# Fused attention and expert layer: the first group's keys cast and turned tile by tile, and a score visit moved ahead of the value pass

## The chip, the cores and the metric

The kernel runs on one core of a Trainium2 chip. The metric is the device time of one execution, in microseconds (us). Engines: PE (TensorE, matmuls), DVE (VectorE), ACT (ScalarE), POOL (GpSimd, here also the queue of most loads) and SP (SyncE, the queue of the first loads and of the stores). A matmul's weight load is listed apart, as PEld.

## The reference

The inputs q, k and v have shape 8 x 12 x 448 x 64 (batch, heads, sequence, head dimension), in float32. Attention uses a sigmoid in place of a softmax; its output goes through an expert layer with a gated hidden width of 2048:

```python
scores = scale * np.matmul(q, k.transpose(0, 1, 3, 2)) - np.log(S)
attn = 1.0 / (1.0 + np.exp(-scores))
attn_out = np.matmul(attn, v)
x = attn_out.transpose(0, 2, 1, 3).reshape(B * S, H * D)      # 3584 x 768
h = x @ w_in                                                  # 768 -> 2048
out = (h * (1.0 / (1.0 + np.exp(-beta * h)))) @ w_out         # 2048 -> 768
```

## The kernel before, in words

**Tiling.** The 12 heads of a batch form three groups of four heads; a group g holds its queries and keys as one tile `raws[g]` of 128 partitions (4 heads x 32 rows), two halves (queries, keys) and 14 chunks of 64 columns. A DVE transpose in 32 x 32 blocks of 32-bit words (L191 to L210) turns queries into `qT[g]` and keys into `kT[g]`, with pairs of fp16 numbers as words. The 448 keys of a head are three tiles of 128 (jt 0, 1, 2) and a last one of 64 (jt 3, `JF`); chunk c of the first twelve belongs to tile c mod 3, so a key tile is four chunks of 64 numbers, three chunks apart. A slot is two heads; a group has two slots.

**The opening** (L708 to L810, a schedule written out by hand: each engine runs its instructions in the order of the program). Two SP loads bring the first half of group 0's queries and all of its keys as float32 into the still unused tile `gt` (L723); everything else comes over POOL's queue, cast to fp16 by the DMA: queries and keys of groups 1 and 2, the values of batch 0 (L136, L143), the second halves of the queries, then the weights w_in (L153). DVE casts and turns group 0's queries (L747, L196). Of its keys ACT casts the second 448 columns (L749) and DVE the first (L750), and one transpose turns tiles 0 to 2 (384 words, L204), another the last tile (64 words, L208).

`half_visit(g, c0, second)` (L256) makes the scores of one half of the queries (224 columns from c0) of one group: with `second` 0 the key tiles 0 and 1, with 1 the tiles 2 and 3. It takes two score tiles (one for each slot, two PSUM banks each) out of a pool of three, runs 16 matmuls (L218) that go tile by tile, and two sigmoids on ACT (`weigh`, L230) write the weights. `attend(g, c0, n, part)` (L279) multiplies these weights by the values: 8 matmuls a slot (L291) into one PSUM bank a slot, out of two banks that `bank` (L89) gives out, the least recently used first; a DVE copy then writes `xT` (L300) and frees the bank. `double_v_last` (L145) is a DVE copy that the value pass needs. `idle_units` (L738) are matmuls of 512 columns on zeros, whose result nobody reads.

The order is: 10 idle units and one of 256 columns; six half visits for the first query half (groups 0, 1, 2), with 4, 4, 4, 4 and 2 idle units between them; `double_v_last`; the transpose of the second query half of group 0; then `attend(0)`, half visit (0, second query half, 0), `attend(1)`, half visit (0, second query half, 1), the other query transposes, and `attend(2)` slot by slot (L767 to L781). Four transposes turn beta (L784). Then the score pool is closed and opened again with two tiles, which leaves four banks for the expert layer (L794, L795), whose first matmuls (`dense1`, L305, L171) need the `xT` of all six slots and sigmoids with beta (L317). From there on a written list of steps (`STEPS`) mixes the attention of later batches with the expert layer.

Of the kernel before, what the change touches and what calls it, by code (L numbers as in the profile page):

```python
# [8 lines left out]
FP32 = mybir.dt.float32  # L9
FP16 = mybir.dt.float16  # L10
# [3 lines left out]
def kernel(  # L14
# [10 lines left out]
    nc = tc.nc  # L25
# [3 lines left out]
    B, H, S, D = q.shape  # L29
    NTOK, DM = out.shape  # L30
    DFF = moe_w_in.shape[1]
    P = 128
    BLK = 32
    HQ = P // BLK
    NB = S // BLK
    PAIR = D // BLK
    JF = S // P
    KL = S - JF * P
    NF = JF * P // BLK
    NPAIR = H // 2  # L40
    QPB = H // HQ
# [5 lines left out]
    QH = S // 2  # L47
# [7 lines left out]
    vp = ctx.enter_context(tc.tile_pool(name="vp", bufs=2))  # L55
    qTp = ctx.enter_context(tc.tile_pool(name="qTp", bufs=3))
    kTp = ctx.enter_context(tc.tile_pool(name="kTp", bufs=3))
# [27 lines left out]
    def touch(i: int):  # L85
        used[i] = max(used.values()) + 1


    def bank(name: str, cols: int = S, hold=None):  # L89
        i = min((i for i in used if i not in held.values()), key=used.get)  # L90
        touch(i)
        if hold is not None:
            held[hold] = i
        pool = psum["one" if i < N_ONE else "late"]
        return pool.tile([P, cols], FP32, tag=f"one{i}", name=name)
# [12 lines left out]
    raws = {}  # L108
    vs = {}
# [19 lines left out]
    def last_base(s: int) -> int:  # L129
        return (s % 2 ^ swapped(s // 2)) * KL  # L130

    def load_v(b: int):
        vs[b] = vp.tile([P, H, JF + 1, D], FP16, tag="v16", name="v16")
        rows = v[b].rearrange("h (p c) d -> p h (c d)", c=NB)
        for i in range(HQ):
            nc.gpsimd.dma_start(  # L136
                out=vs[b][i * BLK : (i + 1) * BLK, :, 0:JF].rearrange("p h j d -> p h (j d)"),
                in_=rows[:, :, JF * i * D : JF * (i + 1) * D],
            )
        rows = v[b].rearrange("h (p c) d -> p h c d", c=NB)  # L140
        for c in range(NF, NB):
            lo = (c - NF) * BLK
            nc.gpsimd.dma_start(out=vs[b][lo : lo + BLK, :, JF], in_=rows[:, :, c])  # L143

    def double_v_last(b: int):  # L145
        nc.vector.tensor_copy(out=vs[b][KL:P, :, JF], in_=vs[b][0:KL, :, JF])

    WCH = 8
    WOUT = 2
# [30 lines left out]
    kT = {}  # L180
# [10 lines left out]
    def transpose(g: int, r: int, c0: int = 0, c1: int = NB):  # L191
        raw = raws[g][:, r]
        if r == 0:
            if g not in qT:
                qT[g] = qTp.tile([P, NB * BLK, PAIR], FP16, tag="qT", name="qT")
            nc.vector.transpose(  # L196
                out=in_order(g // QPB, qT[g][:, c0 * BLK : c1 * BLK]),
                in_=raw[:, c0:c1].rearrange("p c d -> p (c d)").bitcast(FP32),
            )
            return  # L200
        kT[g] = kTp.tile([P, S, PAIR], FP16, tag="kT", name="kT")
        to = kT[g].rearrange("p k e -> p (k e)").bitcast(FP32)
        frm = raw.rearrange("p c d -> p (c d)").bitcast(FP32).rearrange("p (c f) -> p c f", c=NB)
        nc.vector.transpose(  # L204
            out=to[:, 0 : JF * P].rearrange("p (j i q) -> p i j q", j=JF, i=HQ),
            in_=frm[:, 0:NF].rearrange("p (i j) f -> p i j f", j=JF),
        )
        nc.vector.transpose(  # L208
            out=to[:, JF * P :], in_=frm[:, NF:].rearrange("p c f -> p (c f)")
        )  # L210
# [45 lines left out]
    def half_visit(g: int, c0: int, second: int):  # L256
        slots = (2 * g, 2 * g + 1)
        scos = [score_tile() for _ in slots]
        plan = [(s, jt, sco, jt * QH) for jt in (0, 1) for s, sco in zip(slots, scos)]
        widths = [S, S]  # L260
        if second:
            plan = [(s, 2, sco, 0) for s, sco in zip(slots, scos)]
            plan += [(s, JF, scos[0], QH) for s in slots]
            widths = [S, QH]
        for i in range(0, len(plan), 2):
            for e in range(PAIR):
                for s, jt, sco, u0 in plan[i : i + 2]:
                    for hh in range(2):
                        score(sco, u0, s, jt, hh, e, c0, QH)
        homes = [None, None]  # L270
        if c0 == 0 and g < QPB - 1:
            home = outp.tile([P, 2 * S], FP32, tag="osb", name="early")
            home = home.bitcast(FP16).rearrange("p (x h s) -> p x h s", x=2, h=2)
            homes = [home[:, x] for x in range(2)]
        ats = {id(sco): weigh(sco, n, at) for sco, n, at in zip(scos, widths, homes)}
        for s, jt, sco, u0 in plan:
            at_tiles[s, jt, c0] = ats[id(sco)][:, :, u0 : u0 + QH]
# [430 lines left out]
    NH = NB // 2  # L708
# [4 lines left out]
    with tc.manual_schedule():  # L713
        raws[0] = rawp.tile([P, 2, NB, D], FP16, tag="raw", name="raw")
        wide = gt.rearrange("p a b -> p (a b)").bitcast(FP32)
        cut = NH * D
        early = [(0, 0, NH), (1, 0, NB)]
        staged = {}
        at = 0
        for r, c0, c1 in early:  # L720
            staged[r] = wide[:, at : at + (c1 - c0) * D]
            at += (c1 - c0) * D
            nc.sync.dma_start(  # L723
                out=staged[r],
                in_=(q, k)[r][0, 0:HQ].rearrange("h (p c) d -> (h p) (c d)", c=NB)[
                    :, c0 * D : c1 * D
                ],
            )
        nc.gpsimd.memset(dummy, 0.0)
        nc.scalar.activation(out=dummy, in_=dummy, func=AF.Sigmoid, bias=0.0, scale=1.0)  # L730

        still = gt[:, NDC - 1, 0:512]
        nc.vector.memset(still, 0.0)
        beta_in = sigp.tile([P, S], FP32, tag="sg", name="beta_in")[0:BLK, 0:P]
        nc.vector.memset(beta_in, 0.0)
        idle = bank("idle_ps", 512)

        def idle_units(n: int, cols: int = 512):  # L738
            for _ in range(n):
                nc.tensor.matmul(  # L740
                    idle[:, 0:cols], still[:, 0:P], still[:, 0:cols], start=True, stop=True
                )

        idle_units(10)
        idle_units(1, 256)
        raw = raws[0].rearrange("p r c d -> p r (c d)")
        nc.vector.tensor_copy(out=raw[:, 0, 0:cut], in_=staged[0])  # L747
        transpose(0, 0, 0, NH)
        nc.scalar.copy(out=raw[:, 1, cut:], in_=staged[1][:, cut:])  # L749
        nc.vector.tensor_copy(out=raw[:, 1, 0:cut], in_=staged[1][:, 0:cut])  # L750
        transpose(0, 1)
        for g in range(1, QPB):
            load_one(g, 0, 0, NH)
            load_one(g, 1)
        load_v(0)
        nc.sync.dma_start(out=beta_in[0:NDC], in_=moe_beta.rearrange("(c p) -> c p", p=P))
        for g in range(QPB - 1):
            load_one(g, 0, NH, NB)
        for c in range(WCH):
            if c == WCH // 2:  # L760
                load_one(QPB - 1, 0, NH, NB)
            load_w_in(c)
        for g in range(1, QPB):
            transpose(g, 0, 0, NH)
            transpose(g, 1)

        for g in range(QPB):  # L767
            for second in range(2):
                half_visit(g, 0, second)
                if 2 * g + second < 2 * QPB - 1:  # L770
                    idle_units(4 if g < QPB - 1 else 2)
        double_v_last(0)
        transpose(0, 0, NH, NB)
        attend(0, 0, QH)
        half_visit(0, QH, 0)
        attend(1, 0, QH)
        half_visit(0, QH, 1)
        for g in range(1, QPB - 1):
            transpose(g, 0, NH, NB)
        attend(2, 0, QH, (0,))  # L780
        attend(2, 0, QH, (1,))  # L781
        for i in range(P // BLK):
            part = slice(i * BLK, (i + 1) * BLK)
            nc.vector.transpose(out=beta_sb[part], in_=beta_in[:, part])  # L784
        load_qk(QPB)
        load_qk(QPB + 1)
        load_v(1)
        load_w_out(0, 0)
        load_w_out(1, 0)
        load_qk(QPB + 2)  # L790
        load_w_out(0, 1)
        load_w_out(1, 1)

        firsts.close()  # L794
        share_psum(ctx, seconds, 2, N_ONE, 2)  # L795
        first_half(4)
        half_visit(1, QH, 0)
        first_half(3)
        half_visit(1, QH, 1)
        transpose(2, 0, NH, NB)  # L800
        attend(0, QH, QH)
        first_half(1)
        half_visit(2, QH, 0)
        first_half(4)
        half_visit(2, QH, 1)
        attend(1, QH, QH)
        first_half(3)
        attend(2, QH, QH)
        first_half(1)
        follow(STEPS)  # L810
# [30 lines left out]
```

## Time and profile before

| | us |
|---|---|
| median of 3 runs | 368.29 (367.94 to 368.37) |
| profiled execution, device time | 368.51 |
| profiled execution, span from first to last instruction | 366.7 |
| PE busy | 361.6 |
| ACT busy | 248.7 |
| DVE busy | 271.7 |
| last landing of group 0's keys (L723), ACT and DVE start on them | 4.76 |
| first score matmul (L218) | 6.00 |
| first sigmoid (L230) | 6.66 |
| first expert matmul (L171) | 19.42 |

A line of the timeline gives the start in us from the start of the span, the busy time in us, engine, line, operation, output<-input, shapes, the number of instructions merged into it, and in brackets the idle time of the engine just before with what ended it. A line of the chain gives start, length and what the time was spent on; "issue" is time in which the engine waited for nothing that the profile shows. The granted TensorE clock is 1.000 over the span.

### The profile page before, as it was taken

To read this page: it belongs to the slowest core of one execution; us is meant where nothing else is said; L and a number is where in the kernel's file an instruction comes from. 1 tells how busy PE (TensorE), PEld (TensorE's weight loads), DVE (VectorE), ACT (ScalarE), POOL (GpSimd) and SP (SyncE) were. 2 spreads that over 40 slices of the span, in tenths; PEclk is the share of its full clock that TensorE was granted. 3 is DMA by queue.
4 is the path that set the end of the run, shared out by engine and by line. 5 is a ranking of instruction groups with operands and counts; after the bars stand their busy time and mean duration, and the time that the engine had idled before them with its cause. 6 is when DMAs were issued, how large, how long until landed. Compare 5 with 4: busy or idle time off the path is not lost.

```text
span 366.7 us, 9126 instructions
## 1 busy us (share of the span) xinstructions
PE 361.6 (99%) x3677; PEld 238.0 (65%) x3677; DVE 271.7 (74%) x521; ACT 248.7 (68%) x409; POOL 154.3 (42%) x192
## 2 busy tenths in 40 slices
PE   8999999999999999999999999999999999999996
PEld 3478754457465685557857667666856687679763
DVE  3356569889995796876778678868878667678764
ACT  4987976789765797657865579977874859226410
POOL 7834523504413873117761445841630316316610
PEclk9999999999999999999999999999999999999999
DMA  8999999930363790416919363373303030030234
GB/s 168 184 197 201 199 206 198 236 39 2 50 139 52 160 152 2 74 64 111 156 13 149 52 137 52 49 81 89 52 1 89 2 88 2 0 88 0 56 68 138
DMA packets 42698, 34.76 MB, mean 95 GB/s; under 512 B 21904, under 2 KB 39200, under 8 KB 42656
## 3 DMA queue, kind: packets, MB, share of 16 engines
q0 software_dynamic: 36688, 22.47, 44.8%
q1 hardware_dynamic: 5968, 11.71, 11.5%
q8 instruction: 29, 0.48, 0.6%
q14 instruction: 13, 0.11, 0.1%
HBM read 45.62 MB, written 11.01 MB: 154 GB/s over the span
## 4 chain that ended last, share of the span: by engine, by line
PE 93%; DMA 3%; ACT 2%; DVE 1%; SPq 0%; issue 0%; ACTq 0%; DVEq 0%
PE m_ps L171 71%; PE sco L218 12%; PE av_ps L291 9%; DMA out_dram<-osb 2%; ACT attnT L230 1%; PE idle_ps L740 1%; DMA gt<-in_k_dram 1%; DVE osb L372 0%; SPq L602 0%; ACT osb L425 0%; DVE xT L300 0%; DVE kT L204 0%; ACT raw L749 0%; ACT osb L463 0%; SPq L723 0%
## 5 line engine op out<-in xcount | busy, mean ns | idle before, releaser
L230 ACT ACTIVATE attnT<-sco 128x896 f16<-128x896 f32 (+1 forms) x163 | 139.2, 908 | 37.8 <-PE sco L218 37.1
L372 DVE TENSOR_TENSOR osb<-m_ps,osb 128x448 f32<-128x448 f32 (+2 forms) x197 | 116.3, 596 | 51.1 <-PE m_ps L171 42.0
L171 PEld LDWEIGHTS <-w_in 128*128 128x128 f16 (+1 forms) x948 | 81.0, 100 | 18.8 <-issue 11.0
L171 PE MATMUL m_ps<-xT,w_in 128*128 128x224 f16 (+3 forms) x750 | 85.5, 266 | 0.3 <-ACT attnT L230 0.2
L492 POOL TENSOR_TENSOR gt<-osb,sg 128x448 f16<-128x448 f32 x26 | 29.5, 1135 | 117.8 <-ACT sg L425 107.7
L502 POOL TENSOR_TENSOR gt<-osb,sg 128x448 f16<-128x448 f32 x52 | 58.3, 1138 | 35.1 <-ACT sg L425 33.5
L425 ACT ACTIVATE sg<-osb,beta_sb 128x224 f32<-128x224 f32 (+1 forms) x104 | 54.0, 575 | 10.3 <-DVE osb L372 10.0
L171 PEld LDWEIGHTS <-sum 128*128 128x128 f16 (+1 forms) x444 | 39.9, 99 | 27.4 <-issue 3.6
L171 PEld LDWEIGHTS <-gt 128*128 128x128 f16 (+1 forms) x474 | 36.9, 102 | 25.7 <-issue 7.5
L171 PE MATMUL m_ps<-w_out,gt 128*128 128x384 f16 (+2 forms) x350 | 52.6, 324 | 0.0
L218 PE MATMUL sco<-qT,kT 32*128 32x448 f16 (+3 forms) x864 | 51.5, 340 | 0.3 <-ACT attnT L230 0.2
L171 PEld LDWEIGHTS <-w_S 128*128 128x128 f16 (+1 forms) x486 | 43.9, 99 | 7.0 <-issue 6.0
L171 PE MATMUL m_ps<-w_out,sum 128*128 128x384 f16 (+1 forms) x228 | 40.6, 327 | 0.0
L171 PE MATMUL m_ps<-w_T,sum 128*128 128x384 f16 (+1 forms) x216 | 40.3, 326 | 0.0
L300 DVE CAST xT<-av_ps 128x448 f16<-128x448 f32 (+1 forms) x54 | 28.4, 566 | 14.2 <-PE av_ps L291 14.1
L291 PE MATMUL av_ps<-attnT,v 128*64 128x448 f16 (+3 forms) x400 | 38.2, 343 | 0.0
L171 PE MATMUL m_ps<-xs,w_S 128*128 128x224 f16 (+1 forms) x330 | 36.2, 259 | 0.0
L291 PEld LDWEIGHTS <-v 128*64 128x64 f16 (+1 forms) x432 | 20.4, 108 | 17.7 <-issue 9.8
L425 ACT ACTIVATE osb<-m_ps,beta_sb 128x224 f32<-128x224 f32 x52 | 20.4, 448 | 15.4 <-PE m_ps L171 15.1
L218 PEld LDWEIGHTS <-kT 32*128 32x128 f16 (+1 forms) x864 | 13.5, 96 | 23.1 <-issue 21.5
L320 DVE TENSOR_TENSOR gt<-m_ps,sg 128x224 f16<-128x224 f32 (+1 forms) x40 | 16.6, 434 | 12.5 <-ACT sg L317 12.2
L463 ACT COPY osb<-m_ps 128x448 f32<-128x448 f32 x26 | 13.8, 535 | 17.7 <-PE m_ps L171 15.5
(50 smaller groups left out, 303.5 us busy)
## 6 DMA issues: line engine op xcount, KB each, us to landing
out_dram<-osb SPq DMA_DIRECT2D x100, 96.0 KB, 2.4
raw<-in_k_dram POOLq DMA_DIRECT2D x23, 224.0 KB, 5.7
raw<-in_q_dram POOLq DMA_DIRECT2D x21, 224.0 KB, 4.4
v<-in_v_dram POOLq DMA_DIRECT2D x32, 144.0 KB, 7.0
w_in<-in_moe_w_in_dram POOLq DMA_DIRECT2D x8, 384.0 KB, 10.3
w_out<-in_moe_w_out_dram POOLq DMA_DIRECT2D x4, 768.0 KB, 13.1
v<-in_v_dram POOLq DMA_DIRECT2D x16, 48.0 KB, 6.4
out_dram<-osb SPq DMA_DIRECT2D x4, 192.0 KB, 2.4
```

What stands on the lines that cost most here:

```text
L171: nc.tensor.matmul(to[c : c + step], hidden[:, c : c + step], weights, **({} if step == P else {"tile_position": (0, c)}), **flags,)
L218: nc.tensor.matmul(sco[base : base + nk, hh, u0 : u0 + n], kT[g][lo : lo + BLK, jt * P : jt * P + nk, e], qT[g][lo : lo + BLK, c0 : c0 + n ...
L230: nc.scalar.activation(out=at[:, :, 0:n], in_=sco[:, :, 0:n], func=AF.Sigmoid, bias=NEG_LOG_S, scale=MSCALE,)
L291: nc.tensor.matmul(av[hh * D : (hh + 1) * D, 0:n], vs[b][base : base + nk, 2 * (s % NPAIR) + hh, jt], at[base : base + nk, hh, 0:n], start ...
L300: nc.vector.tensor_copy(out=xTs[b][:, s % NPAIR, c0 : c0 + n], in_=av[:, 0:n])
L320: nc.vector.tensor_tensor(out=gt[:, dc, off : off + n], in0=m1[:, 0:n], in1=sg[:, 0:n], op=ALU.mult)
L372: nc.vector.tensor_tensor(out=out, in0=in0, in1=in1, op=op)
L425: nc.scalar.activation(out=out, in_=in_, func=AF.Sigmoid, bias=0.0, scale=beta_sb[:, dc : dc + 1])
L463: nc.scalar.copy(out=oa[:, 0], in_=m)
L492: nc.gpsimd.tensor_tensor(out=gt[:, 2 * d : 2 * d + 2, off : off + QH], in0=ob[:, 0], in1=sg, op=ALU.mult)
L502: nc.gpsimd.tensor_tensor(out=gt[:, dc, off : off + S].rearrange("p (h n) -> p h n", h=2), in0=oa[:, :, j], in1=sg, op=ALU.mult,)
L740: nc.tensor.matmul(idle[:, 0:cols], still[:, 0:P], still[:, 0:cols], start=True, stop=True)
```

## The change

1. Group 0's keys are cast and turned by key tile. ACT casts tile 1 (256 numbers a partition, four runs of 64) and the last 128 columns; DVE casts tile 0, turns tiles 0 and 1 with a transpose of 128 words each, casts tile 2, turns it, and turns the last 64 words. DVE thus has two casts and four transposes where it had one cast and two transposes; ACT has two casts where it had one. PE's first score matmul waits for the transpose of tile 0, the ninth for that of tile 1.
2. Half visit (0, second query half, 0) is put ahead of `attend(0)`, and its sibling ahead of `attend(1)`; `attend(1)` and `attend(2)` then follow each other. The transpose of the second query half of group 0 is put ahead of `double_v_last` on DVE.
3. Idle units: 9 and one of 256 columns at the start (before 10 and one), and 3, 4, 4, 4, 3, 2 behind the six half visits (before 4, 4, 4, 4, 2 and none). Each call of `idle_units` takes a bank by `bank`, where one bank was used throughout.
4. `load_v` and `double_v_last` are rewritten with a helper `move_v` and heads from h0 on; they are called with h0 = 0, and issue the same DMAs and the same copy.

The order of POOL's and SP's instructions is unchanged. The diff, without the rewriting of `load_v`:

```diff
-        idle_units(10)
+        idle_units(9)
         idle_units(1, 256)
         raw = raws[0].rearrange("p r c d -> p r (c d)")
         nc.vector.tensor_copy(out=raw[:, 0, 0:cut], in_=staged[0])
         transpose(0, 0, 0, NH)
-        nc.scalar.copy(out=raw[:, 1, cut:], in_=staged[1][:, cut:])
-        nc.vector.tensor_copy(out=raw[:, 1, 0:cut], in_=staged[1][:, 0:cut])
-        transpose(0, 1)
+        whole = [
+            t[:, 0 : NF * D].rearrange("p (i j d) -> p i j d", j=JF, d=D)
+            for t in (staged[1], raw[:, 1])
+        ]
+        kT[0] = kTp.tile([P, S, PAIR], FP16, tag="kT", name="kT")
+        words = kT[0].rearrange("p k e -> p (k e)").bitcast(FP32)
+
+        def key_cast(copy, j: int):
+            copy(out=whole[1][:, :, j], in_=whole[0][:, :, j])
+
+        def key_turn(j: int):
+            nc.vector.transpose(
+                out=words[:, j * P : (j + 1) * P].rearrange("p (i q) -> p i q", i=HQ),
+                in_=raws[0][:, 1, 0:NF]
+                .rearrange("p c d -> p (c d)")
+                .bitcast(FP32)
+                .rearrange("p (i j q) -> p i j q", i=HQ, j=JF)[:, :, j],
+            )
+
+        key_cast(nc.scalar.copy, 1)
+        nc.scalar.copy(out=raw[:, 1, NF * D :], in_=staged[1][:, NF * D :])
+        key_cast(nc.vector.tensor_copy, 0)
+        key_turn(0)
+        key_turn(1)
+        key_cast(nc.vector.tensor_copy, 2)
+        key_turn(2)
+        nc.vector.transpose(out=words[:, JF * P :], in_=raw[:, 1, NF * D :].bitcast(FP32))
...
-        for g in range(QPB):
-            for second in range(2):
-                half_visit(g, 0, second)
-                if 2 * g + second < 2 * QPB - 1:
-                    idle_units(4 if g < QPB - 1 else 2)
+        for n in range(2 * QPB):
+            half_visit(n // 2, 0, n % 2)
+            idle_units((3, 4, 4, 4, 3, 2)[n])
+        transpose(0, 0, NH, NB)
         double_v_last(0)
-        transpose(0, 0, NH, NB)
-        attend(0, 0, QH)
         half_visit(0, QH, 0)
+        attend(0, 0, QH)
+        half_visit(0, QH, 1)
         attend(1, 0, QH)
-        half_visit(0, QH, 1)
         for g in range(1, QPB - 1):
             transpose(g, 0, NH, NB)
         attend(2, 0, QH, (0,))
```

More of the change, by code (lines that the diff above doesn't have):

```diff
@@ L130, in last_base, with move_v, load_v, double_v_last @@
         return (s % 2 ^ swapped(s // 2)) * KL
-    def load_v(b: int):
-        vs[b] = vp.tile([P, H, JF + 1, D], FP16, tag="v16", name="v16")
-        rows = v[b].rearrange("h (p c) d -> p h (c d)", c=NB)
+    def move_v(queue, to, b: int, h0: int, h1: int):
+        rows = v[b, h0:h1].rearrange("h (p c) d -> p h (c d)", c=NB)
         for i in range(HQ):
-            nc.gpsimd.dma_start(
-                out=vs[b][i * BLK : (i + 1) * BLK, :, 0:JF].rearrange("p h j d -> p h (j d)"),
+            queue.dma_start(
+                out=to[i * BLK : (i + 1) * BLK, h0:h1, 0:JF].rearrange("p h j d -> p h (j d)"),
                 in_=rows[:, :, JF * i * D : JF * (i + 1) * D],
             )
-        rows = v[b].rearrange("h (p c) d -> p h c d", c=NB)
+        rows = v[b, h0:h1].rearrange("h (p c) d -> p h c d", c=NB)
         for c in range(NF, NB):
             lo = (c - NF) * BLK
-            nc.gpsimd.dma_start(out=vs[b][lo : lo + BLK, :, JF], in_=rows[:, :, c])
-    def double_v_last(b: int):
-        nc.vector.tensor_copy(out=vs[b][KL:P, :, JF], in_=vs[b][0:KL, :, JF])
+            queue.dma_start(out=to[lo : lo + BLK, h0:h1, JF], in_=rows[:, :, c])
+    def load_v(b: int, h0: int = 0):
+        vs[b] = vp.tile([P, H, JF + 1, D], FP16, tag="v16", name="v16")
+        move_v(nc.gpsimd, vs[b], b, h0, H)
+    def double_v_last(b: int, h0: int = 0):
+        nc.vector.tensor_copy(out=vs[b][KL:P, h0:, JF], in_=vs[b][0:KL, h0:, JF])
     WCH = 8
@@ L735 @@
         nc.vector.memset(beta_in, 0.0)
-        idle = bank("idle_ps", 512)
         def idle_units(n: int, cols: int = 512):
+            idle = bank("idle_ps", 512)
             for _ in range(n):
@@ L765 @@
             transpose(g, 1)
-        for g in range(QPB):
-            for second in range(2):
-                half_visit(g, 0, second)
-                if 2 * g + second < 2 * QPB - 1:
-                    idle_units(4 if g < QPB - 1 else 2)
+        for n in range(2 * QPB):
+            half_visit(n // 2, 0, n % 2)
+            idle_units((3, 4, 4, 4, 3, 2)[n])
+        transpose(0, 0, NH, NB)
         double_v_last(0)
-        transpose(0, 0, NH, NB)
+        half_visit(0, QH, 0)
         attend(0, 0, QH)
-        half_visit(0, QH, 0)
+        half_visit(0, QH, 1)
         attend(1, 0, QH)
-        half_visit(0, QH, 1)
         for g in range(1, QPB - 1):
```

## The prediction

> **What bounds the kernel now.** I read the page's busy times first, then the chain of work that ended last over the whole span, then that chain for 4.5 to 20 us (the diff touches only what runs before the first expert matmul), then the timelines of ACT, PE and DVE there. The page says PE:
>
> ```profile
> PE 361.6 (99%) x3677; PEld 238.0 (65%) x3677; DVE 271.7 (74%) x521; ACT 248.7 (68%) x409; POOL 154.3 (42%) x192
> PE 93%; DMA 3%; ACT 2%; DVE 1%; SPq 0%; issue 0%; ACTq 0%; DVEq 0%
> ```
>
> From the first expert matmul (L171, 19.42) to the end PE hardly stops: after that time the waits of PE show no wait for another engine. So the end moves by as much as that stage's steady start moves, one for one. Before it, the chain for 4.5 to 20 us reads
>
> ```profile
> 4.76 0.57 ACT raw L749
> 5.33 0.03 issue
> 5.36 0.59 DVE kT L204
> 5.95 0.05 issue
> 6.00 0.62 PE sco L218 x16
> 6.62 0.97 PE idle_ps L740 x4
> ...
> 16.29 3.08 ACT attnT L230 x4
> 19.37 0.04 issue
> 19.42 0.64 PE m_ps L171 x5
> ```
>
> The keys' cast and transpose release the first scores, then PE and ACT hand work to each other, and ACT's last sigmoid releases the expert stage. I call the half visits h0 to h7 (h0 to h5: first query half of groups 0 to 2; h6, h7: second half of group 0) and the value passes of the first query half a0, a1, a2. ACT's timeline shows that it sets the pace:
>
> ```profile
> 6.66 6.28 ACT L230 ACTIVATE early<-sco 128x896 f16<-128x896 f32 x8 [1.33 <-PE sco L218]
> 13.08 6.29 ACT L230 ACTIVATE attnT<-sco 128x896 f16<-128x896 f32 x8
> ```
>
> Four groups of two half visits, 3.21 us each (6.66, 9.87, 13.08, 16.29), ended by 19.37. And the PE timeline shows how a0 to a2 lie between scores:
>
> ```profile
> 14.05 0.69 PE L218 MATMUL sco<-qT,kT 32*128 32x224 f16 x14 [0.18 <-ACT attnT L230]
> 14.67 0.99 PE L291 MATMUL av_ps<-early,v 128*64 128x224 f16 x16
> 15.59 0.75 PE L218 MATMUL sco<-qT,kT 32*128 32x224 f16 x16
> 16.27 1.06 PE L291 MATMUL av_ps<-early,v 128*64 128x224 f16 x16
> 17.26 0.70 PE L218 MATMUL sco<-qT,kT 32*128 32x224 f16 x16
> 17.89 1.31 PE L291 MATMUL av_ps<-attnT,v 128*64 128x224 f16 x16
> 19.42 1.31 PE L171 MATMUL m_ps<-xT,w_in 128*128 128x224 f16 x12 [0.21 <-ACT attnT L230]
> ```
>
> That is h5, a0, h6, a1, h7, a2: each value pass fills time in which the next scores would wait for ACT anyway.
>
> **Part 1: the keys, a gain d.** Before: ACT's 448-element cast 4.76 to 5.33 (0.56), DVE's 384-column transpose 5.36 to 5.94 (0.58), PE at 6.00. Now the first transpose has 128 columns and waits for a 256-element cast on each engine. ACT's cast: sigmoids of 896 and 448 elements took 0.917 and 0.538, so 0.85 ns an element; 192 fewer give 0.40 (proportional 0.32, no shorter 0.56). DVE's cast (0.39 for 448) ends before that. Transposes of 64, 224 and 384 columns took 0.20, 0.41 and 0.58; 128 columns about 0.29 (not below 0.20). So: 4.76 + 0.40, 0.03 to the start as before, 5.20 to 5.49, and PE 0.06 behind, at 5.55: 0.45 earlier. The ends: 0.56 with 0.29 gives 5.71 (0.29 earlier), 0.32 with 0.20 gives 5.38 (0.62 earlier). The idle matmuls ahead stop in time: one 0.43 unit fewer of 4.66 us in all.
>
> The second tile's transpose ends 0.21 behind the first, at 5.70; PE wants it at 5.81 (0.26 after its start, as now). The third tile's cast, its transpose and the last 64 columns follow by 6.47; h1 wants them near 6.95. Group 1's queries then turn at 6.40 instead of 5.99, ahead of its keys, which wait for a DMA until 7.46. ACT's extra tail cast (128 elements, under 0.3) ends near 5.4, ahead of the first sigmoid. All free, with 0.1 us or more of cover.
>
> The row that speaks against a full 0.45 is PE's own: idle matmuls of 512 columns start every 0.43 us up to 5.43, and every 0.216 us from 6.55; within h0 the first four scores stand 0.16 apart from the next four, the later fours 0.10. PE speeds up near 6.1, and 0.45 of h0 would now run ahead of that. At the slow rate its steps of four take 0.19: up to 0.20 lost. So d lies between 0.09 and 0.62; I take 0.35, between 0.25 (speeds up at the same moment) and 0.45 (does not matter).
>
> [...]
>
> **Part 2: h6 ahead of a0.** What can h6 start with? Three score buffers: h6's second tile takes that of h5's first, which ACT leaves at 15.71; its third matmul ran at 15.76 and its first sigmoid at 16.29, 0.58 after the release. h2 and h4, with no value pass ahead, show the same 0.58 (9.29 to 9.87, 12.50 to 13.08). So a0 did not delay h6, and moving h6 gains ACT nothing; it would only save the 0.2 or so that the values cost once all is d earlier (their copy on DVE, L146, ended at 14.51, as late as their DMA allows). DVE's query transpose now precedes that copy: its load's last landing is at 14.26, so 14.29 to 14.70; h6 cannot use it before 15.76 - d. Nothing else queues there.
>
> What is late next: a1 and a2 now both follow h7. In times of before, all to be taken d earlier:
> - h5 leaves PE at 14.67; two idle units to 15.20; h6 goes on at 15.76 and leaves PE at 16.27.
> - a0 16.27 to 17.19 (0.92 as from 14.67 to 15.59), its last matmul done 17.26; DVE's two copies 17.29 to 17.98 (0.69 for two).
> - h7's third matmul waits for ACT's release at 17.21: 17.26, PE free at 17.89, as before. ACT ends at 19.37, as before.
> - a1 from 17.89; its second bank needs a0's second copy: third matmul 18.03, PE free 0.82 later, 18.86, done 18.92; copies 18.96 to 19.35 and to 19.65.
> - a2 needs the first of these banks (there are two, and a1 holds both): 19.40. Before, h7 lay over that wait. Its two slots take 0.62 each (17.89, 18.51, 19.13): second slot 20.02, PE free 20.64. Its last copy began 0.74 after the slot's start (18.51 to 19.25): 20.76 to 21.15.
> - Expert matmuls from 20.64; the sixth needs that copy: 21.20, against 19.89 before.
>
> So 1.31 us later, less d. Of it 0.54 is the copy wait; were it hidden, 0.77 would be left. The two extra idle units (20 behind the visits, 18 before) lie in waits for ACT, the one fewer behind h0 too: h1's third matmul waits for ACT either way. Behind 21.20 nothing catches up: beta's transposes (0.84) follow the last copy as now, and the weights' DMAs, unmoved, only gain cover.
>
> **Sum.** 1.31 - 0.35 = +0.96. The profiled execution took 368.51 (366.7 span and 1.8 around it), so 369.47; the median 368.29 lies 0.22 lower: 369.25, say 369.2. From the ends of d: +0.69 to +1.22, 368.98 to 369.51.
>
> **Rivals.**
> - *ACT alone sets the stage's start.* Then the values are off the path and only d shows: 19.42 - 0.35, that is 367.94 (367.67 for 0.62). For it: ACT is busy without a break from 6.66 to 19.37. Against: it decides only if a1 and a2 end by ACT's end; from 17.89 there are 1.48 us, and they need 2.75 (1.93 without the copy wait). Beyond that point PE decides. It would need a d above 0.74 as well to come out over 0.2% faster. Chance 0.1.
> - *PE speeds up late.* If it stays at the slow rate past 8 us, the idle units between h0 and h1 become the path: 4 x 0.43 before, 3 x 0.43 now. Before, h1 goes on at 8.46 instead of 7.62; after, at 7.59: d is 0.87, and the change costs 0.44: 368.7. For it: the slow rows end only at 5.43. Against: in this profile they were over by 6.55. [...] Chance 0.2.
> - *The tilewise keys bring nearly nothing* (ACT's cast no shorter, h0 slow): +1.22 and some more wait, 369.5 to 369.8. Chance 0.1.
> - My forecast: 0.6.
>
> 0.2% is 0.74 us, about what a measurement of this kernel can tell from no change. The forecast falls mostly above +0.74, its corner with d over 0.57 below. Faster 0.06 (the first rival, with PE late to speed up), same 0.29, slower 0.65. The range, with the late gate and most of the unknown ends, is 368.2 to 369.8.
>
> **What would show it.** The first sigmoid at 6.2 to 6.4 instead of 6.66; eight groupwise starts 3.21 apart as before; ACT's last sigmoid of h7 at about 19.0; on PE h6, a0, h7, a1, a gap of half a us that ends with a DVE copy, a2, and the sixth expert matmul near 20.85. Wrong if PE shows no such gap, if h6's first sigmoid comes less than 0.58 after the release, or if the expert stage starts with ACT's end.

## The result and the profile after

| | before | after |
|---|---|---|
| median of 7 runs, us | 368.35 (367.94 to 368.74) | 369.42 (368.81 to 369.97) |
| ratio, after to before | | 1.0028, 95% interval 1.0016 to 1.0040 |
| profiled execution and its span, us | 368.51, 366.7 | 369.42, 367.5 |
| ACT and DVE start on the keys | 4.76 | 4.93 |
| first score matmul, first sigmoid | 6.00, 6.66 | 5.73, 6.52 |
| end of h7's last sigmoid | 19.37 | 19.22 |
| first and sixth expert matmul | 19.42, 19.89 | 20.51, 21.06 |
| from the first sigmoid to the sixth expert matmul | 13.24 | 14.55 |

The change is slower by 1.07 us; 0.96 was forecast. The names h0 to h7 and a0 to a2 are those of the prediction; times in text that no shown line has are starts of single instructions in the trace.

The page of the changed kernel, engines and then the chain of work that ended last:

```profile
PE 361.9 (98%) x3678; PEld 238.2 (65%) x3678; DVE 271.8 (74%) x524; ACT 248.6 (68%) x410; POOL 154.2 (42%) x192
PE 96%; ACT 1%; DMA 1%; DVE 0%; issue 0%; SPq 0%
```

PE has nearly the same work (361.9 us against 361.6) and is idle for 5.6 us of its span, against 5.1 before. That the share of DMA in the chain fell from 3% to 1% belongs to a store much later, which the account of the prediction comes to. The chain from 4 to 24 us (start, length, what) shows the opening:

```profile
4.93 0.41 ACT raw L760
5.34 0.02 issue
5.37 0.32 DVE kT L763
5.69 0.05 issue
5.73 0.80 PE sco L221 x15
...
17.81 1.02 PE av_ps L294 x16
18.84 0.38 DVE xT L303
19.22 0.04 issue
19.26 1.31 PE av_ps L294 x16
```

Before, cast and transpose held PE for 1.24 us behind the landing (4.76 to 6.00); now it is 0.80. But the end of this stage is no longer ACT: a DVE copy stands between two value passes, and the expert matmuls follow a2. ACT's timeline has moved as a block, 0.14 earlier, with the same length:

```profile
6.52 6.28 ACT L233 ACTIVATE early<-sco 128x896 f16<-128x896 f32 x8 [0.98 <-PE sco L221]
12.94 6.28 ACT L233 ACTIVATE attnT<-sco 128x896 f16<-128x896 f32 x8
```

PE's timeline is the one to lay beside that of before:

```profile
14.53 0.60 PE L743 MATMUL idle_ps<-gt 128*128 128x512 f16 x2
15.07 0.27 PE L221 MATMUL sco<-qT,kT 32*128 32x224 f16 x2
15.62 0.57 PE L221 MATMUL sco<-qT,kT 32*128 32x224 f16 x14 [0.28 <-ACT attnT L233]
16.13 0.99 PE L294 MATMUL av_ps<-early,v 128*64 128x224 f16 x16
17.05 0.77 PE L221 MATMUL sco<-qT,kT 32*128 32x224 f16 x16
17.74 1.04 PE L294 MATMUL av_ps<-early,v 128*64 128x224 f16 x16
19.26 1.31 PE L294 MATMUL av_ps<-attnT,v 128*64 128x224 f16 x16 [0.48 <-DVE xT L303]
20.51 2.54 PE L174 MATMUL m_ps<-xT,w_in 128*128 128x224 f16 x24
```

h6 stands ahead of a0 and still goes on at 15.62, when ACT lets go of its tile; in that place PE had a0 before, now it has idle units and a wait. a1 and a2, 2.8 us with the wait between them, follow h7, while ACT is done at 19.22.

### The profile page after: what moved, and what is told of

The parts are those of the page before. It is cut to its first block, busy times and chain, and to the rows that moved or that the text cites. A ratio compares the mean times of both kernels' runs of the same rounds, so it can differ in the third digit from the quotient of the medians.

```text
span 367.5 us, 9131 instructions
## 1 busy us (share of the span) xinstructions
PE 361.9 (98%) x3678; PEld 238.2 (65%) x3678; DVE 271.8 (74%) x524; ACT 248.6 (68%) x410; POOL 154.2 (42%) x192
## 4 chain that ended last, share of the span: by engine, by line
PE 96%; ACT 1%; DMA 1%; DVE 0%; issue 0%; SPq 0%
PE m_ps L174 74%; PE sco L221 12%; PE av_ps L294 10%; DMA gt<-in_k_dram 1%; PE idle_ps L743 1%; ACT attnT L233 1%; ACT early L233 0%; ACT raw L760 0%; SPq L726 0%; DVE xT L303 0%; DVE osb L375 0%; DVE kT L763 0%
```

## The experiments

The theory (the expectations call it the stack theory): the order of PE's work costs 1.31 us ahead of the expert stage, less what the keys gain. The rival: ACT's end sets the start of that stage, the order is free, and the loss has another source. Each kernel was timed beside the kernel before on the same chip.

**Keys alone.** The order and the idle units behind the visits are put back, and all idle units use one bank again:

```diff
-            idle_units((3, 4, 4, 4, 3, 2)[n])
-        transpose(0, 0, NH, NB)
+            idle_units((4, 4, 4, 4, 2, 0)[n])
         double_v_last(0)
-        half_visit(0, QH, 0)
+        transpose(0, 0, NH, NB)
         attend(0, 0, QH)
-        half_visit(0, QH, 1)
+        half_visit(0, QH, 0)
         attend(1, 0, QH)
+        half_visit(0, QH, 1)
```

> Only the keys by tile (and 9 full idle units at the start instead of 10); order of visits and value passes, order of the query transpose and the value copy on DVE, and idle units behind the visits as before. Stack theory (the loss is a1 and a2 behind h7): no loss is left and d shows, first sigmoid 0.15 to 0.35 ahead of before, sixth expert matmul at 19.55 to 19.75 (19.89 before, 21.06 after), 0.15 to 0.35 us faster than before. Rival (ACT's end sets the expert stage, so the order costs nothing and the keys or the slow first visit bring the loss): about as slow as the changed kernel, +1.1 us.

368.69 against 368.53, ratio 1.0007 (0.9993 to 1.0021): nothing that can be measured; the 0.15 to 0.35 us that were expected are not confirmed. In the profile the sixth expert matmul comes at 19.74, 13.23 behind the first sigmoid, and the stage begins with ACT's end again (chain of waits):

```profile
16.14 3.08 ACT attnT L233 x4
19.22 0.04 issue
19.26 1.79 PE m_ps L174 x17
```

So the loss is not in the keys; their gain is 0.15 in this profile, too small for the measured time, whose interval is about 0.5 us wide to either side.

**Order alone.** Kernel before, with the moved lines of the change and the idle units of before:

> Only the order (h6 ahead of a0, h7 ahead of a1, the query transpose ahead of the value copy); keys and all idle units as before. Stack theory: sixth expert matmul 1.31 us later than before, at 21.2, ACT's sigmoids at the old times, +1.3 us. Rival (ACT's end sets the stage): equal to before.

370.45 against 368.53, ratio 1.0059 (1.0036 to 1.0082). One of these six executions, the profiled one, took 1258.29 us, with idle units of 0.80 us; the five others have a median of 370.25. The second time:

> Only the order, again (the profiled execution of the first run had its matmuls at a quarter of their rate all through, so its trace is of no use). Counted from the first sigmoid of h0 to the sixth expert matmul: 13.23 before, 14.54 in the changed kernel. Stack theory: 14.54, with the first sigmoid at the time of before, +1.3 us. Rival (ACT's end sets the expert stage): 13.23, no loss.

369.97 against 368.87, ratio 1.0031 (1.0020 to 1.0041): slower, which excludes the rival. But the trace had 15.87 from the first sigmoid to the sixth expert matmul, 1.33 more than the theory gave. The busy time by stretches (stretch, its length, busy time and instructions of PE, PEld, DVE, ACT and POOL, granted clock, DMA share, GB/s) shows where:

```profile
14.00:15.00 1.00, 0.76 (x16) 0.33 (x11) 0.21 (x1) 1.00 (x2) 1.00 (x2) 1.00 1.43 189
15.00:16.00 1.00, 0.49 (x14) 0.31 (x13) 0.00 (x0) 0.90 (x2) 1.00 (x2) 1.00 1.46 196
16.00:17.00 1.00, 1.00 (x14) 0.92 (x12) 0.00 (x0) 0.96 (x2) 0.37 (x2) 0.53 1.44 187
17.00:18.00 1.00, 1.00 (x16) 0.27 (x12) 0.29 (x1) 0.77 (x1) 0.72 (x1) 0.50 1.42 190
18.00:19.00 1.00, 1.00 (x18) 0.57 (x16) 0.40 (x2) 0.27 (x1) 0.00 (x0) 0.50 1.45 198
19.00:20.00 1.00, 0.99 (x16) 0.71 (x11) 0.00 (x0) 1.00 (x2) 0.55 (x1) 0.76 1.45 196
```

This kernel has no idle units between h5 and h6. PE stood still for half of 15 to 16, and then the clock was at half, by the trace's clock records from 16.06 to 19.47: a0, h7 and a1 took 1.59, 1.00 and 1.87 from start to next start, against 0.92, 0.70 and 1.52 in the changed kernel, 1.32 more together. Over the two measurements of this kernel, three of the fifteen executions other than that of 1258.29 us read a mean granted clock of 0.993 to 0.995 and took 370.65 to 371.87 us; the twelve others read 0.998 or more and took 369.10 to 370.40. So it is not the fall that puts the medians above that of before. The next kernel adds only the two units:

```diff
-                if 2 * g + second < 2 * QPB - 1:
-                    idle_units(4 if g < QPB - 1 else 2)
+                idle_units(4 if g < QPB - 1 else 2)
```

> Only the order, with keys as before and two idle units behind h5, as in the changed kernel (the kernel with the order alone had none there, and its granted clock fell to half from 16 to 19.3). Theory (order costs 1.31, and the clock fell because PE stood idle around 15): granted clock 1.00 from 14 to 20, 14.54 from the first sigmoid to the sixth expert matmul, 1.3 us slower than before. Rival (the order itself costs more than 1.31, the idle units are without effect): 15 or more, with the clock falling again.

369.91 against 368.42, ratio 1.0032 (1.0019 to 1.0045). The granted clock is 1.00 in each of these stretches, and 14.55 came out, as in the changed kernel. Its PE timeline:

```profile
15.84 0.57 PE L218 MATMUL sco<-qT,kT 32*128 32x224 f16 x14 [0.28 <-ACT attnT L230]
...
19.48 1.31 PE L291 MATMUL av_ps<-attnT,v 128*64 128x224 f16 x16 [0.48 <-DVE xT L300]
20.73 1.48 PE L171 MATMUL m_ps<-xT,w_in 128*128 128x224 f16 x13
```

ACT's last sigmoid of h7 ended at 19.44 and the expert stage began 1.29 later. That settles the order: 1.31 (14.55 less 13.24), and the rival falls. The keys by tile and a bank for each call of `idle_units`, which only the changed kernel has, add nothing to this count. The two swapped DVE instructions were not tried alone; in the changed kernel they are done at 14.69, and a0 starts at 16.13. That the two idle units keep the clock up is not shown: the six executions with them read 0.999 or more, but so did twelve of the fifteen without them, or nearly (0.998).

**The copy wait inside it.** a2 gets banks that nobody holds. First both from one score tile:

```diff
-        attend(2, 0, QH, (0,))
-        attend(2, 0, QH, (1,))
+        spare = score_tile()
+        attend(2, 0, QH, (0,), [spare[:, 0]])
+        attend(2, 0, QH, (1,), [spare[:, 1]])
```

> The changed kernel with a2's two PSUM banks taken from the third score tile, which ACT has left by then, instead of the two banks that a1 holds. Stack theory: the half us in which PE waits for a copy between a1 and a2 goes, sixth expert matmul at 20.5 to 20.6 instead of 21.06, 0.5 us faster than the changed kernel, still 0.5 to 0.7 slower than before. Rival (ACT's end sets the stage): as the changed kernel.

369.72 against 368.53, ratio 1.0049 (1.0032 to 1.0066): the expectation failed, with 14.82 from the first sigmoid to the sixth expert matmul. The wait had only moved; PE's timeline:

```profile
18.34 0.69 PE L294 MATMUL sco<-attnT,v 128*64 128x224 f16 x8
19.78 0.69 PE L294 MATMUL sco<-attnT,v 128*64 128x224 f16 x8 [0.75 <-DVE xT L303]
```

The first slot starts right behind a1, but the second slot, in the other bank of the same tile, waited 0.75 us for the first slot's copy. With the second slot in its old place (`attend(2, 0, QH, (1,))`):

> The changed kernel with only the first slot of a2 in the free score tile; its second slot takes the bank that a1's first copy frees meanwhile. Stack theory: no wait between a1 and a2's slots, 14.0 from the first sigmoid to the sixth expert matmul instead of 14.54, half a us faster than the changed kernel and 0.4 to 0.6 slower than before. If the copies are not what PE waits for: 14.54.

```profile
18.34 0.69 PE L294 MATMUL sco<-attnT,v 128*64 128x224 f16 x8
18.96 0.69 PE L294 MATMUL av_ps<-attnT,v 128*64 128x224 f16 x8
19.59 1.58 PE L174 MATMUL m_ps<-xT,w_in 128*128 128x224 f16 x14
```

No wait is left, 13.99 from the first sigmoid to the sixth expert matmul, 0.56 less than the changed kernel. 369.04 against 368.87, ratio 1.0006 (0.9995 to 1.0017): with the keys' gain the loss is within what can be measured, and smaller than the 0.4 to 0.6 expected. In this profile PE was fast early, the first sigmoid came 0.50 ahead of before, and the sixth expert matmul 0.25 behind it. So of 1.31 the copy wait was 0.56, and the rest is PE work put behind h7.

**The idle units.**

> The changed kernel with the idle units behind the visits as before (4, 4, 4, 4, 2, none). If they lie in waits for ACT, as the prediction had it, nothing changes: 14.5 from the first sigmoid to the sixth expert matmul, time as the changed kernel, except that a slow start of PE may cost 0.2 at the fourth unit behind h0. If the two units behind h5 or the third behind h4 delay the next visit: up to 0.4 faster than the changed kernel.

369.68 against 368.87, ratio 1.0023 (1.0013 to 1.0033). 14.73 from the first sigmoid, of which 0.18 is a slow fourth unit behind h0; PE's timeline:

```profile
5.43 0.94 PE L221 MATMUL sco<-qT,kT 32*128 32x224 f16 x16
6.29 1.32 PE L743 MATMUL idle_ps<-gt 128*128 128x512 f16 x4
```

Here scores and idle units ran slow until 6.9. The other units lay in waits; the clock did not fall later, though PE was busy for only 0.37 of 15 to 16.

**The score tiles turned by one place.** The kernel with only the keys by tile, and a second `score_tile()` ahead of the schedule.

> As the kernel with only the keys by tile, with the three score tiles turned by one place (one more tile taken and left unused ahead of the schedule), so that h7 uses other score tiles. If the first expert matmul waits for ACT only because its bank lies under a tile of h7, it now starts when a2 leaves PE, 0.2 to 0.3 earlier, and the last copy lets the sixth go at about 19.45: 0.4 us faster than before. If it needs ACT's end anyhow: as the kernel with only the keys by tile.

368.28 against 368.53, ratio 1.0002 (0.9991 to 1.0013). The first expert matmul waited 0.2 for ACT as before: the rotation does not decide it. Which release it needs stays open.

**The opposite order.** h7 behind the first three expert tiles, keys by tile:

```diff
-        first_half(4)
+        first_half(3)
+        half_visit(0, QH, 1)
+        first_half(2)
         half_visit(1, QH, 0)
```

> The opposite of the change: keys by tile, old order for h6, and h7 taken behind the first three expert tiles, so that a1 and a2 (first slot in the free score tile) run as soon as h6 is done; the expert tiles between the later visits are dealt 3, 2, 3, 1, 3 instead of 4, 3, 1, 4. Stack theory: what PE does ahead of the expert stage decides, so the sixth expert matmul comes at 12.4 to 12.6 from the first sigmoid, 0.7 less than before; h7 costs 0.6 later on, and with the keys' gain the whole is 0.2 to 0.5 faster than before, if ACT keeps up with the visits that now stand closer. Rival (ACT sets the pace everywhere): waits for ACT at the later visits eat it, equal to before or slower.

The sixth expert matmul came at 18.58, 12.40 from the first sigmoid, as forecast by the theory. 368.51 against 368.87, ratio 0.9992 (0.9978 to 1.0006): no measurable gain, where 0.2 to 0.5 us were expected. In the profile it is 1.31 ahead of before at 18.58; the sigmoids behind it, paired by order, are 0.32 ahead at 42 and 0.21 at 75 us. 0.63 of that is h7 itself (19.92 to 20.55); where the rest went was not followed. No version tried beats the kernel before beyond the interval.

## Why the prediction was right

- **The order, 1.31 less d**: right to the hundredth; 1.31 with the order alone, 1.31 in the change. It was built from starts of before alone, and each stood: h6 0.58 behind ACT's release, a1's second bank waiting for a0's second copy, a2 waiting for a1's first (0.48 idle), the sixth matmul on the last copy. The copy wait was put at 0.54, counted from when PE could have gone on; its idle time in the timeline is 0.48, and taking it out gained 0.56.
- **Casts and transposes**: ACT's cast 0.41 (0.40 forecast), the first transpose 0.32 (0.29), PE 0.80 behind the landing (0.79).
- **d**: the term that was mis-sized: 0.14 in this profile instead of 0.35, inside 0.09 to 0.62. The signs that hang on it missed by as much: the first sigmoid at 6.52 instead of 6.2 to 6.4, ACT's end at 19.22 instead of 19.0, the sixth expert matmul at 21.06 instead of 20.85. The median moved by 1.07, as a d of 0.24 would have it. Two parts: the keys landed 0.17 later than in before's profile, which the change does not explain (4.52 to 4.93 over ten profiles, with whole and with tilewise casts alike), and h0 ran slow (its steps of four 0.17, 0.19 and 0.13; the first sigmoid 0.79 behind PE's start instead of 0.66). Over the kernels with tilewise keys the first sigmoid came 1.42 behind the landing where PE was already fast (three profiles), and 1.59 to 1.85 where not (four); with whole casts 1.85 to 1.89 (three). So the keys are worth about 0.45 with a fast PE, as worked out, and nothing to 0.3 without. In two of the slow ones the keys had landed early (4.55 and 4.60), and the idle units ahead, which ran until 5.43, held h0 by 0.07 and 0.02: they do not always stop in time.
- **Idle units cost nothing**: right as far as their time goes, but the one profile in which the clock fell, at a cost of 1.33, was of a kernel without the two behind h5. The prediction did not name that.
- **Nothing catches up behind**: right up to 160 us: sigmoids paired by order are 1.17 later from 28 us on, as the stage starts. But the two profiles end 0.8 apart, so the end did not move one for one: before's had a stall of about 0.48 that this one had not. Its chain goes through a store at 171.03 (5.74 us to landing), then ACT, then PE at 181.21. The profile of the kernel with the turned score tiles had that stall as well, and an earlier one, a store at 152.01 (7.12 us to landing) and then DVE, which put it back by 0.49. Waits for such stores make part of the differences between profiles.
- **Rivals**: ACT alone setting the stage fell. The argument against it has a wrong figure: without the copy wait a1 and a2 need 2.21 by the prediction's own rows (2.75 less 0.54), not 1.93, and without that wait they took 2.21 (17.38 to 19.59); either is above the 1.48 us that are left. A PE that speeds up late was seen twice, at a cost of 0.15 and 0.18 behind h0 rather than the 0.87 of a wholly slow stretch. The range counted with a slow rate past 8 us; over ten profiles, all but that of 1258.29 us, none shows it, and the latest doubling of PE's rate was at 6.90.

## What to carry to other kernels

Where a slow engine sets the pace and another fills its waits, moving work for the pacing engine forward gains nothing if that work cannot start before a buffer comes free; the filler that stood in the wait then lands at the end, on the path (here at a cost of 1.31 us). List what each wait was filled with before moving anything out of it, and look for a bank that two passes share once they become neighbours. A gain of 0.15 to 0.45 us in the first 6 us of a 368 us kernel is seen in a trace and not in its time.

## What the runs showed of the hardware

The idle matmuls begin at 1.19 in the profiles, but the time at which PE doubles its rate (from 0.43 us to 0.216 a unit) ranged from about 4.0 to 6.9 over the ten profiles without that of 1258.29 us. The view's granted clock reads 1.00 all through that, but the clock records in the traces begin only at the doubling (6.14 in the profiles before and after, 3.96 at the earliest, 6.90 at the latest), so the 1.00 ahead of it is not a measurement. What sets that moment these profiles do not show.

With the order alone the clock also fell to half behind two stretches of 1 us in which PE was busy for 0.76 and 0.49; with the idle units as before it did not fall behind 0.88 and 0.37. The fall lasted 3.41 us (16.06 to 19.47). In the 3.41 us ahead of it PE was busy for 2.48, and its longest idle time there was 0.63; with the idle units as before it was busy for 2.48 as well in a stretch of the same length (13.73 to 17.14), and the clock did not fall. What decides between the two stays open.
